# U, the masks and V0 in the opening of a convolution and low-rank mixer kernel, on one Trainium2 core

## The chip, the core and the metric

The kernel runs on one core of one Trainium2 chip. The core has five engines with an instruction stream each: TensorE (PE in the profile, with its weight loads shown apart as PEld), VectorE (DVE), ScalarE (ACT), GpSimd (POOL) and SyncE (SP). Data comes from device memory by transfers; in this kernel POOL issues nearly all loads (the queue "software_dynamic" of the profile), SP issues the transposes and the stores (the queue "hardware_dynamic"). The metric is the device time of one execution in microseconds (us). Durations of profiled instructions below are in us too.

## What is computed

x is 8 x 4224 x 192 float32. A causal convolution of seven taps comes first, with softmax weights for each of eight heads of 24 columns, and then a mixer: a product of rank 32 along the sequence, and a two-layer network along the columns.

```python
def _attn_ref(x, weight):                     # B, S, D = 8, 4224, 192; H, K = 8, 7
    w = exp(weight - max(weight)); w = w / (sum(w) + 1e-09)
    out = np.einsum('hk,bskhg->bshg', w, x_unf)      # K shifted views of x, heads of 24 columns

def _moe_ref(x, U, V, w_ch1, w_ch2):          # x is the convolution's output
    xt = x.transpose(0, 2, 1)
    h = xt @ U @ V                            # U is 4224 x 32, V is 32 x 4224
    u = x + h.transpose(0, 2, 1)
    ch = np.maximum(u @ w_ch1, 0.0) @ w_ch2   # 192 -> 768 -> 192
    return (u + ch).astype(np.float32)
```

## The kernel before

The kernel's order of work is written out by hand. Each batch of 4224 positions is 33 tiles of 128 positions; eight tiles make a group, 33 groups in all. For each group w1 multiplies by the first weight (L561, with ReLU evictions at L575 on ACT and L577 on DVE), w2 by the second (L590), and the result is added to u and stored (L599, L607). SLOTS is the list that lays the rest (convolutions of later batches, their sums with U, their products with V, transposes) between these products. None of that is touched by the change.

What is touched is the opening, the first 22 us, in which batch 0 is brought to its first group. In the order of PE:

- idle (L155) multiplies a tile of zeros by itself in float32, with no reader: one call has n products of w times 128 columns.
- The softmax weights become `cm` (8 x 7 x 8), which a product with the ones `one8` (L201) spreads to all 128 partitions. A copy makes `c2` of it (L218), two DVE products make `pr` (L226), and band_half (L241) sums these with the identity into a bank, from which ACT and DVE copy the band matrices (L261, L263: evac, on the engine that its letter names).
- The convolution of batch 0 comes in four pieces, KP, since x comes in four loads (x_piece, L79): conv_piece(k) needs piece k of x. Its products are L376, its evictions to y_sb are L261 and L263.
- u_layout (L269) puts U, loaded as four rows to a partition (Ur, L123 and L127), into U_sb by sixteen small products with the mask Eq; four evictions follow. It waits for both loads of Ur, for Eq, and for four free banks.
- yT (L514) transposes y of a group by a product with the identity, into three banks y0 that stay open.
- tt_mm (L409) sums y times U over the tiles of batch 0 into the bank tp; tt_split, a sum with R4 (L768), tt_late (L689) for the last piece, and tt_done make tt_sb of it.
- hT (L529) adds V times tt_sb to the open banks: three parts c of 64 columns, each with its own copy of the first 2048 columns of V, in the partitions 32c to 32c + 31 of V0_sb. Then it evicts the three banks as uT (ACT, DVE, ACT), which w1 of the groups 0 and 1 reads.

POOL's stream of transfers before: x piece 0, x piece 1, Ur, the rest of Ur, x pieces 2 and 3, three times V0 (L134), four parts of W1 (L138), then the first part of batch 1's x, V_sb, W2 and the rest of batch 1. At most eight of POOL's transfers are open: each further one waits for the landing of the one eight places before it. SP's stream before: the softmax weights (L61), and then nothing until the first transpose (L505).

The masks fp, R4 and Eq (L711, L714, L718) are made on DVE after yT of the first group. `early` are the 27 tiles of the pieces 0 to 2 (10, 11 and 6 of them); tt_mm takes them in two stretches, 21 and 6, before and after the first part of piece 3.

In the profile's lines the numbers are left off tile names: V_sb stands for V0_sb too, W_sb for W1_sb and W2_sb, and R for R4.

Of the kernel before, what the change touches and what calls it, by code (L numbers as in the profile page):

```python
# [7 lines left out]
ALU = mybir.AluOpType  # L8
ACT = mybir.ActivationFunctionType
BF16 = mybir.dt.bfloat16  # L10
F32 = mybir.dt.float32
# [3 lines left out]
def kernel(  # L15
# [10 lines left out]
    nc = tc.nc  # L26
    P = nc.NUM_PARTITIONS
    B, S, D = x.shape
    H, KC = weight.shape
    GS = D // H  # L30
    R = moe_U.shape[1]
# [4 lines left out]
    GT = 8  # L36
# [8 lines left out]
    cst = ctx.enter_context(tc.tile_pool(name="cst", bufs=1))  # L45
# [10 lines left out]
    def bank():  # L56
        return psp.tile([P, 512], F32, name="ps", tag="ps")
# [12 lines left out]
    def x_tile(b):  # L70
        xt[b] = xs.tile([P, NB1 + 1, D], BF16, name="x_sb")
# [4 lines left out]
    def x_part(b, r, s0, s1):  # L76

        blk = NB0 * r + s0 - 1
        return nc.gpsimd.dma_start(  # L79
            out=xt[b][HB * r : HB * r + HB, s0:s1, :],  # L80
            in_=x[b, blk * HB : (blk + s1 - s0) * HB, :].rearrange("(j p) d -> p j d", p=HB),
        )
# [3 lines left out]
    KP = [(0, 0, 10), (1, 0, 10), (1, 10, NB1 // 2), (0, 10, NB0 // 2)]  # L86

    def x_piece(k):
        r, k0, k1 = KP[k]
        x_part(0, r, 1 - r if k0 == 0 else 2 * k0 + 1, 2 * k1 + 1)  # L90

    def piece_tiles(k):
        r, k0, k1 = KP[k]
        return [NB0 // 2 * r + j for j in range(k0, k1)]
# [9 lines left out]
    def iota(t, pattern, base, mul):  # L104
# [4 lines left out]

    fp = cst.tile([P, P], I32, name="fp")  # L110
    nc.gpsimd.iota(fp[:], pattern=[[1, P]], base=P, channel_multiplier=-1)
    x_piece(1)
    dif = cst.tile([P, BW], F32, name="dif")
    iota(dif[:], [[1, BW]], 0, -1)
    tap = cst.tile([P, KC], F32, name="tap")
# [8 lines left out]
        out=Ur[:, 0:nfull, :], in_=U4[0 : nfull * P, :].rearrange("(k p) c -> p k c", p=P)  # L124
    )
    nlast = NT * 32 - nfull * P
    nc.gpsimd.dma_start(out=Ur[0:nlast, nfull, :], in_=U4[nfull * P :, :])  # L127
    for k in range(2, len(KP)):
        x_piece(k)


    V0_sb = cst.tile([3 * R, 2 * GT * P], BF16, name="V0_sb")
    for c in range(3):
        nc.gpsimd.dma_start(out=V0_sb[R * c : R * c + R, :], in_=moe_V[:, 0 : 2 * GT * P])  # L134
    W1_sb = cst.tile([P, 3, M4], BF16, name="W1_sb")
    for m0, m1 in ((0, 2 * P), (2 * P, M4)):
        for hf in range(2):
            nc.gpsimd.dma_start(  # L138
                out=W1_sb[HB * hf : HB * hf + HB, :, m0:m1],
                in_=moe_w_ch1[:, m0:m1].rearrange("(c k) m -> k c m", k=HB),  # L140
# [8 lines left out]
    Eq = cst.tile([P, P + 4], BF16, name="Eq")  # L149
# [3 lines left out]
    def idle(n, w=4, p=wps):  # L153
        for _ in range(n):
            nc.tensor.matmul(  # L155
                out=p[:, 0 : w * P].rearrange("p (n t) -> p n t", t=P),
                lhsT=zz[:],
                rhs=zz[:].unsqueeze(1).to_broadcast([P, w, P]),
                start=True,
                stop=True,  # L160
            )

    for w in (4, 2, 1):
        idle(1, w)
    one8 = cst.tile([H, P], F32, name="one8")
    nc.vector.memset(one8[:], 1.0)

    HQ = H // 2
# [1 line left out]
    for hh in range(2):  # L170
# [6 lines left out]
        out=d_sb[:], in0=w_sb[:], in1=mx_sb[:].to_broadcast([H, KC]), op=ALU.subtract  # L177
# [3 lines left out]
        out=ident[:], in0=fp[:], scalar1=float(P), scalar2=None, op0=ALU.is_equal  # L181
# [6 lines left out]
    nc.vector.tensor_scalar_add(s2_sb[:], s_sb[:], 1e-9)  # L188
    rs_sb = cst.tile([H, 1], F32, name="rs_sb")
    nc.vector.reciprocal(rs_sb[:], s2_sb[:])  # L190
    cm = cst.tile([H, KC, H], F32, name="cm")
    nc.vector.scalar_tensor_tensor(
        out=cm[:],
        in0=e_sb[:].unsqueeze(2).to_broadcast([H, KC, H]),
        scalar=rs_sb[:, 0:1],
        in1=ident[0:H, 0:H].unsqueeze(1).to_broadcast([H, KC, H]),
        op0=ALU.mult,
# [4 lines left out]
        out=cb[:, 0 : 2 * KC * HQ].rearrange("p (a k h) -> p a k h", a=2, k=KC),  # L202
# [7 lines left out]
        out=hot[:],  # L210
        in0=dif[:].unsqueeze(1).to_broadcast([P, KC, BW]),
        scalar=rq[:, 0:1],
        in1=tap[:].unsqueeze(2).to_broadcast([P, KC, BW]),
        op0=ALU.add,
# [4 lines left out]
        out=c2[:].rearrange("p a k h d -> p (a k h) d"),  # L219
        in_=cb[:, 0 : 2 * KC * HQ].unsqueeze(2).to_broadcast([P, 2 * KC * HQ, 2]),  # L220
    )
    prs = []
    for hh in range(2):
# [3 lines left out]
            out=pr[:].rearrange("p k h (t d) -> p k h t d", d=2),  # L227
            in0=hot[:]
# [4 lines left out]
            op=ALU.mult,  # L233
        )

    R4 = cst.tile([P, P], BF16, name="R4")

    def band_half(hh):
# [20 lines left out]
    def evac(eng, out, in_):  # L259
        if eng == "A":  # L260
            nc.scalar.activation(out=out, in_=in_, func=ACT.Copy)  # L261
        else:
            nc.vector.tensor_copy(out=out, in_=in_)  # L263

    def u_layout(up):
        nb = [nfull + (1 if 32 * jj < nlast else 0) for jj in range(4)]
        for a in range(4):
            for jj in range(4):
                nc.tensor.matmul(  # L269
                    out=up[jj][:, 0 : nb[jj] * R],  # L270
                    lhsT=Eq[32 * jj : 32 * jj + 32, 3 - a : 3 - a + P],
                    rhs=Ur[32 * jj : 32 * jj + 32, 0 : nb[jj], a * R : (a + 1) * R],
                    start=(a == 0),
                    stop=(a == 3),
                    tile_position=(32 * jj, 0),
                )
        for jj in range(4):
            evac(
                "AD"[jj % 2],
                U_sb[:, 0 : nb[jj], jj, :],  # L280
                up[jj][:, 0 : nb[jj] * R].rearrange("p (k r) -> p k r", r=R),
            )
# [1 line left out]
    idle(1, 2)  # L284
    idle(1, 1)
    band_half(0)
    idle(1, 1)
    band_half(1)


# [112 lines left out]
    def tt_mm(b, js, p=None, n0=0, n1=None):  # L403

        if p is None:
            p = bank()
        for n, j in list(enumerate(js))[n0:n1]:
            c = n % 4
            nc.tensor.matmul(  # L409
                out=p[32 * c : 32 * c + 32, 0:D],  # L410
                lhsT=U_sb[:, j // 4, j % 4, :],
                rhs=yt[b][:, j, :],
                start=(n < 4),
                stop=(n + 4 >= len(js)),
                tile_position=(0, 32 * c),
            )
        return p
# [14 lines left out]
    def tt_sum(b):  # L432
        p = bank()
        for n, part in enumerate(ttb[b]):
            nc.tensor.matmul(
                out=p[:, 0:D],
                lhsT=R4[:],
                rhs=part[:],
# [71 lines left out]
    def yT(g, c, p, i0=0, i1=4):  # L510

        for i in range(i0, i1):
            for hf in range(2):
                nc.tensor.matmul(  # L514
                    out=p[HB * hf : HB * hf + HB, i * P : (i + 1) * P],
                    lhsT=yt[0][:, GT * g + 4 * hf + i, HB * c : HB * c + HB],
                    rhs=ident[:],
                    start=(i == 0),
                    stop=False,
                    tile_position=(0, HB * hf),  # L520
                )
# [175 lines left out]
    def conv_piece(k, ns, engs, ps=None):  # L697
        r, k0, k1 = KP[k]
        nh = 512 // (GS * (k1 - k0))
        for n, h in list(enumerate(range(0, H, nh)))[ns]:  # L700
            conv(0, h, min(nh, H - h), [r], engs[n], {r: (k0, k1)}, ps and {r: ps[n]})

    every = slice(None)
    idle(1, 1)
    conv_piece(0, every, "ADAD")
    work = [bank() for _ in range(4)]
    tp = bank()
    y0 = [bank() for _ in range(3)]
    for c in range(3):
        yT(0, c, y0[c])  # L710
    nc.vector.tensor_scalar(  # L711
        out=fp[:], in0=fp[:], scalar1=R - 1, scalar2=None, op0=ALU.bitwise_and
    )
    nc.vector.tensor_scalar(  # L714
        out=R4[:], in0=fp[:], scalar1=0.0, scalar2=None, op0=ALU.is_equal
    )

    nc.vector.tensor_scalar(  # L718
        out=Eq[:, 3 : 3 + P].rearrange("p (k a) -> p k a", a=4)[:, :, 0],
        in0=fp[:, 0:R],  # L720
        scalar1=0.0,
        scalar2=None,
        op0=ALU.is_equal,
    )

    conv_piece(1, every, "ADAD", work)
    u_layout([tp] + work[:3])
    idle(3, 1, work[3])
    x_tile(1)
    x_zero(1, nc.gpsimd)  # L730
    x_part(1, *XP[0])
# [3 lines left out]
    for q in range(4):  # L735
        src = moe_V[:, 0 : full * 8 * P].rearrange("r (k q t) -> r k q t", q=4, t=2 * P)
        nc.gpsimd.dma_start(
            out=V_sb[32 * q : 32 * q + 32, 0 : 2 * full, :].rearrange(
                "r (k a) t -> r k (a t)", a=2
            ),  # L740
            in_=src[:, :, q, :],
# [3 lines left out]
        out=V_sb[0:32, 2 * (NT // 8), :], in_=moe_V[:, (NT - 1) * P : NT * P]  # L745
# [5 lines left out]
        out=U4_sb[:],  # L751
        in_=U_sb[:]
# [2 lines left out]
        .to_broadcast([P, len(late), 4, R]),  # L755
    )
    early = piece_tiles(0) + piece_tiles(1) + piece_tiles(2)
    na = len(early) - len(piece_tiles(2))
    conv_piece(2, every, "ADA", work)
    tt_mm(0, early, tp, 0, na)  # L760
    last = [work[3], work[0], work[1]]
    ps0 = work[2]
    conv_piece(3, slice(0, 1), "DAD", last)
    tt_mm(0, early, tp, na)
    tt_split(0, tp)
    conv_piece(3, slice(1, 3), "DAD", last)
    for n, part in enumerate(ttb[0]):
        nc.tensor.matmul(out=ps0[:, 0:D], lhsT=R4[:], rhs=part[:], start=(n == 0), stop=False)  # L768
    idle(1, 1, tp)
# [12 lines left out]
    for r in range(4):  # L782
        q = slice(QB * r, QB * r + QB)
        for hh in range(2):
            nc.gpsimd.tensor_copy(
                out=band2[q, HQ * hh : HQ * hh + HQ, :],
                in_=bands[hh][q, :, HB * (r % 2) : HB * (r % 2) + QB],
# [32 lines left out]
    for gs1, gs2, at in SLOTS:  # L820
# [13 lines left out]
        for p in range(npc + 1):  # L834
            for what in at.get(p, []):
                do(what)
            if p < npc:
                g, k = gs2[p // 4], p % 4
# [35 lines left out]
```

## Time and profile before

| | us |
|---|---|
| three runs | 327.41, 326.92, 327.23; median 327.23 |
| the profiled execution | 329.74 |
| its span, first to last instruction | 328.0 |
| PE busy in the span | 321.3 (98%) |
| DVE, ACT, POOL busy | 268.5, 169.6, 142.6 |

The page of the profile gives each engine's busy time, the queues, the chain of work that ended last, and the costliest groups of instructions. In a line of the timeline the first number is the start in us from the span's start, the second the duration of the whole row, then come the engine, the source line, the operation, what it writes and reads, the shape of one instruction and how many the row holds; in brackets is how long the engine was idle before and what ended the wait. In a line of the chain there are the start, the duration and the work. In a line of the transfers there are the tiles, the engine that issues them, how many, the size of one as it is written, and the median time from issue to landing.

### The profile page before, as it was taken

What the parts mean: (1) busy time and instruction counts of PE and PEld (TensorE: products, weight loads), DVE (VectorE), ACT (ScalarE), POOL (GpSimd) and SP (SyncE); (2) the same over time, 40 slices, a digit from 0 to 9 for tenths busy, and PEclk for the clock granted to TensorE, in tenths of its full rate; (3) what the DMA queues carried; (4) which work ended last, traced back from release to release, by engine and by line L of the source; (5) the groups of instructions that cost most, each with busy time, mean ns of one, the idle gap of its engine ahead of it and who ended that gap; (6) DMA issues with size and microseconds to landing.
All of it is one profiled execution on the core that took longest, in us unless ns stands there. A gap on an engine that the chain in (4) does not pass through costs nothing.

```text
span 328.0 us, 9606 instructions
## 1 busy us (share of the span) xinstructions
PE 321.3 (98%) x4006; PEld 226.6 (69%) x4006; DVE 268.5 (82%) x551; ACT 169.6 (52%) x341; POOL 142.6 (43%) x111
## 2 busy tenths in 40 slices
PE   8999999999999999999999999999999999999994
PEld 6866676478567746867864784587797497497494
DVE  5669989984977997897898699789898897896853
ACT  2467634760586198068429707833903902912910
POOL 8376159815993894994389599000000000000000
PEclk9999999999999999999999999999999999999998
DMA  8999994999999999899999989039369169159044
GB/s 100 193 180 175 211 234 106 185 180 184 247 109 190 215 190 136 172 222 159 218 227 155 143 236 197 26 99 248 67 150 246 41 143 254 39 129 257 2 136 155
DMA packets 122875, 53.76 MB, mean 164 GB/s; under 512 B 87664, under 2 KB 122736, under 8 KB 122832
## 3 DMA queue, kind: packets, MB, share of 16 engines
q1 hardware_dynamic: 84400, 38.06, 51.9%
q0 software_dynamic: 38288, 14.99, 40.5%
q8 instruction: 31, 0.51, 0.6%
q14 instruction: 12, 0.10, 0.1%
q10 hardware_dynamic: 144, 0.10, 0.1%
HBM read 29.98 MB, written 25.95 MB: 171 GB/s over the span
## 4 chain that ended last, share of the span: by engine, by line
PE 84%; DMA 4%; DVE 4%; ACT 3%; POOL 2%; issue 0%; SPq 0%; DVEq 0%
PE ps L590 38%; PE ps L561 33%; PE ps L346 3%; DMA out_dram<-out_sb 3%; PE ps L464 2%; DVE u_sb L486 2%; PE ps L155 2%; PE ps L376 2%; PE ps L409 2%; POOL xb_sb L312 2%; ACT rl_sb L575 2%; DMA uT<-u_sb 2%; ACT y_sb L261 1%; DVE out_sb L599 1%; DVE rl_sb L577 1%; ACT uT L261 1%
## 5 line engine op out<-in xcount | busy, mean ns | idle before, releaser
L575 ACT ACTIVATE rl_sb<-ps 128x512 bf16<-128x512 f32 x233 | 124.5, 604 | 109.6 <-PE ps L561 106.3
L590 PE MATMUL ps<-W_sb,rl_sb 128*128 128x192 bf16 x1584 | 141.1, 246 | 0.3
L590 PEld LDWEIGHTS <-rl_sb 128*128 128x128 bf16 x1584 | 128.4, 98 | 11.9 <-issue 11.2
L561 PE MATMUL ps<-uT,W_sb 64*128 64x512 bf16 x1188 | 132.2, 376 | 0.2
L577 DVE TENSOR_SCALAR rl_sb<-ps 128x512 bf16<-128x512 f32 x163 | 105.4, 687 | 15.6 <-PE ps L561 15.3
L561 PEld LDWEIGHTS <-W_sb 64*128 64x128 bf16 x1188 | 64.9, 94 | 63.1 <-issue 4.1
L599 DVE TENSOR_TENSOR out_sb<-ps,u_sb 128x384 f32<-128x384 f32 (+1 forms) x133 | 70.3, 548 | 28.0 <-PE ps L590 24.8
L312 POOL COPY xb_sb<-x_sb 32x3072 bf16<-32x3072 bf16 (+1 forms) x24 | 67.4, 2824 | 0.5
L486 DVE TENSOR_TENSOR u_sb<-y_sb,ps 128x192 bf16<-128x192 bf16 (+1 forms) x168 | 66.2, 458 | 0.0
L300 POOL COPY xb_sb<-x_sb 128x3072 bf16<-128x3072 bf16 x12 | 32.9, 2744 | 46.8 <-DMA x_sb<-in_x_dram 37.2
L261 ACT ACTIVATE y_sb<-ps 128x384 bf16<-128x384 f32 (+4 forms) x88 | 37.7, 517 | 11.5 <-PE ps L346 7.7
L79 POOL DMA_DIRECT2D x_sb<-in_x_dram x32 | 27.1, 850 | 8.7 <-PE ps L464 2.8
L263 DVE CAST y_sb<-ps 128x408 bf16<-128x408 f32 (+5 forms) x38 | 20.4, 576 | 2.4 <-PE ps L376 2.3
L464 PE MATMUL ps<-tt_sb,V_sb 32*128 32x192 bf16 x264 | 13.3, 246 | 0.6 <-DVE out_sb L599 0.3
L346 PE MATMUL ps<-xb_sb,band 64*32 64x384 bf16 x192 | 12.3, 332 | 0.2 <-POOL xb_sb L312 0.2
L346 PE MATMUL ps<-x_sb,band 64*32 64x384 bf16 x192 | 12.0, 332 | 0.0
L464 PEld LDWEIGHTS <-V_sb 32*128 32x128 bf16 x264 | 5.0, 92 | 8.4 <-issue 8.4
L376 PE MATMUL ps<-x_sb,band 64*64 64x240 bf16 (+3 forms) x192 | 9.6, 275 | 0.0
L423 ACT ACTIVATE tt_hi<-ps 128x192 bf16<-128x192 f32 x8 | 2.7, 331 | 12.3 <-PE ps L409 12.3
L376 PEld LDWEIGHTS <-band 64*64 64x64 bf16 x192 | 7.4, 106 | 1.8 <-issue 1.3
L155 PE MATMUL ps<-zz 128*128 128x128 f32 (+2 forms) x22 | 7.5, 480 | 1.1 <-DVE zz L144 1.1
L346 PEld LDWEIGHTS <-band 64*32 64x32 bf16 x384 | 4.7, 89 | 5.5 <-issue 2.6
(68 smaller groups left out, 71.8 us busy)
## 6 DMA issues: line engine op xcount, KB each, us to landing
out_dram<-out_sb SPq DMA_DIRECT2D x131, 192.0 KB, 3.3
x_sb<-in_x_dram POOLq DMA_DIRECT2D x14, 384.0 KB, 6.7
x_sb<-in_x_dram POOLq DMA_DIRECT2D x7, 432.0 KB, 7.9
x_sb<-in_x_dram POOLq DMA_DIRECT2D x7, 408.0 KB, 10.3
x_sb<-in_x_dram POOLq DMA_DIRECT2D x1, 504.0 KB, 8.1
uT<-u_sb SPq DMA_TRANSPOSE x31, 4.4
x_sb<-in_x_dram POOLq DMA_DIRECT2D x1, 480.0 KB, 5.6
V_sb<-in_moe_V_dram POOLq DMA_DIRECT2D x3, 128.0 KB, 9.7
```

What stands on the lines that cost most here:

```text
L79: return nc.gpsimd.dma_start(out=xt[b][HB * r : HB * r + HB, s0:s1, :], in_=x[b, blk * HB : (blk + s1 - s0) * HB, :].rearrange("(j p) d -> ...
L261: nc.scalar.activation(out=out, in_=in_, func=ACT.Copy)
L300: nc.gpsimd.tensor_copy(out=xbt[b][:, s0:s1, :], in_=xt[b][:, s0 + 1 : s1 + 1, :])
L312: nc.gpsimd.tensor_copy(out=xbt[b][q, s0:s1, :], in_=xt[b][q, s0:s1, :])
L346: nc.tensor.matmul(out=pp[r][QB * cg : QB * cg + QB, 0 : nk[r] * GS], lhsT=w[hr], rhs=t[hr, st : st + 2 * nk[r] - 1 : 2, hs], start=True, ...
L464: nc.tensor.matmul(out=banks[pr][:, a * D : (a + 1) * D], lhsT=V_sb[32 * q : 32 * q + 32, (j // 8) * 2 + j % 2, :], rhs=ttb[b][32 * q : 32 ...
L486: nc.vector.tensor_tensor(out=u_group(g)[:, i : i + n, :, hf, :], in0=yt[b][:, run[0] : run[0] + n, :].rearrange("p n (c k) -> p n c k", c=3),
L561: last = nc.tensor.matmul(out=pps[m][hf][:], lhsT=W1_sb[HB * hf : HB * hf + HB, c, m * P : (m + 1) * P], rhs=uTt[g][HB * hf : HB * hf + HB ...
L575: nc.scalar.activation(out=rl[:, m, hf, :], in_=pp[hf][:], func=ACT.Relu)
L577: nc.vector.tensor_scalar_max(out=rl[:, m, hf, :], in0=pp[hf][:], scalar1=0.0)
L590: last = nc.tensor.matmul(out=cps[:, a * D : (a + 1) * D], lhsT=rlt[g][:, m, hf, (i + a) * P : (i + a + 1) * P], rhs=W2_sb[:, m, :], start ...
L599: nc.vector.tensor_tensor(out=o[:, 0:n, :].rearrange("p n (c k) -> p n c k", c=3), in0=cps[:, 0 : n * D].rearrange("p (n c k) -> p n c k", ...
```

## The change

The load of Ur and its rest go ahead of x piece 1 in POOL's stream. V0 is loaded once; its second and third copy are made from the first, inside the on-chip memory, by two transfers that SP issues. The operands of the product that spreads the softmax weights become bfloat16. The idle product between the two band halves goes. On DVE the masks fp and Eq are made ahead of the bands' evictions, and R4 after U's evictions. On PE the layout of U moves from behind the convolution of piece 1 to ahead of yT of the first group; its three idle products (six passes) go, and one comes in ahead of piece 1. The sums with U are taken in three stretches, each ahead of a later piece: the 10 tiles of piece 0 ahead of piece 1, the 11 of piece 1 after piece 2, the 6 of piece 2 where they were. The rest of the program keeps its order on every engine.

```diff
--- before.py
+++ after.py
@@ -109,7 +109,6 @@
 
     fp = cst.tile([P, P], I32, name="fp")
     nc.gpsimd.iota(fp[:], pattern=[[1, P]], base=P, channel_multiplier=-1)
-    x_piece(1)
     dif = cst.tile([P, BW], F32, name="dif")
     iota(dif[:], [[1, BW]], 0, -1)
     tap = cst.tile([P, KC], F32, name="tap")
@@ -125,13 +124,14 @@
     )
     nlast = NT * 32 - nfull * P
     nc.gpsimd.dma_start(out=Ur[0:nlast, nfull, :], in_=U4[nfull * P :, :])
-    for k in range(2, len(KP)):
+    for k in range(1, len(KP)):
         x_piece(k)
 
 
     V0_sb = cst.tile([3 * R, 2 * GT * P], BF16, name="V0_sb")
-    for c in range(3):
-        nc.gpsimd.dma_start(out=V0_sb[R * c : R * c + R, :], in_=moe_V[:, 0 : 2 * GT * P])
+    nc.gpsimd.dma_start(out=V0_sb[0:R, :], in_=moe_V[:, 0 : 2 * GT * P])
+    for c in range(1, 3):
+        nc.sync.dma_start(out=V0_sb[R * c : R * c + R, :], in_=V0_sb[0:R, :])
     W1_sb = cst.tile([P, 3, M4], BF16, name="W1_sb")
     for m0, m1 in ((0, 2 * P), (2 * P, M4)):
         for hf in range(2):
@@ -162,7 +162,7 @@
 
     for w in (4, 2, 1):
         idle(1, w)
-    one8 = cst.tile([H, P], F32, name="one8")
+    one8 = cst.tile([H, P], BF16, name="one8")
     nc.vector.memset(one8[:], 1.0)
 
     HQ = H // 2
@@ -188,7 +188,7 @@
     nc.vector.tensor_scalar_add(s2_sb[:], s_sb[:], 1e-9)
     rs_sb = cst.tile([H, 1], F32, name="rs_sb")
     nc.vector.reciprocal(rs_sb[:], s2_sb[:])
-    cm = cst.tile([H, KC, H], F32, name="cm")
+    cm = cst.tile([H, KC, H], BF16, name="cm")
     nc.vector.scalar_tensor_tensor(
         out=cm[:],
         in0=e_sb[:].unsqueeze(2).to_broadcast([H, KC, H]),
@@ -233,6 +233,16 @@
             op=ALU.mult,
         )
 
+    nc.vector.tensor_scalar(
+        out=fp[:], in0=fp[:], scalar1=R - 1, scalar2=None, op0=ALU.bitwise_and
+    )
+    nc.vector.tensor_scalar(
+        out=Eq[:, 3 : 3 + P].rearrange("p (k a) -> p k a", a=4)[:, :, 0],
+        in0=fp[:, 0:R],
+        scalar1=0.0,
+        scalar2=None,
+        op0=ALU.is_equal,
+    )
     R4 = cst.tile([P, P], BF16, name="R4")
 
     def band_half(hh):
@@ -284,7 +294,6 @@
     idle(1, 2)
     idle(1, 1)
     band_half(0)
-    idle(1, 1)
     band_half(1)
 
 
@@ -706,26 +715,12 @@
     work = [bank() for _ in range(4)]
     tp = bank()
     y0 = [bank() for _ in range(3)]
+    u_layout(work)
+    nc.vector.tensor_scalar(
+        out=R4[:], in0=fp[:], scalar1=0.0, scalar2=None, op0=ALU.is_equal
+    )
     for c in range(3):
         yT(0, c, y0[c])
-    nc.vector.tensor_scalar(
-        out=fp[:], in0=fp[:], scalar1=R - 1, scalar2=None, op0=ALU.bitwise_and
-    )
-    nc.vector.tensor_scalar(
-        out=R4[:], in0=fp[:], scalar1=0.0, scalar2=None, op0=ALU.is_equal
-    )
-
-    nc.vector.tensor_scalar(
-        out=Eq[:, 3 : 3 + P].rearrange("p (k a) -> p k a", a=4)[:, :, 0],
-        in0=fp[:, 0:R],
-        scalar1=0.0,
-        scalar2=None,
-        op0=ALU.is_equal,
-    )
-
-    conv_piece(1, every, "ADAD", work)
-    u_layout([tp] + work[:3])
-    idle(3, 1, work[3])
     x_tile(1)
     x_zero(1, nc.gpsimd)
     x_part(1, *XP[0])
@@ -755,13 +750,16 @@
         .to_broadcast([P, len(late), 4, R]),
     )
     early = piece_tiles(0) + piece_tiles(1) + piece_tiles(2)
-    na = len(early) - len(piece_tiles(2))
+    n1, n2 = len(piece_tiles(0)), len(early) - len(piece_tiles(2))
+    tt_mm(0, early, tp, 0, n1)
+    idle(1, 1, work[3])
+    conv_piece(1, every, "ADAD", work)
     conv_piece(2, every, "ADA", work)
-    tt_mm(0, early, tp, 0, na)
+    tt_mm(0, early, tp, n1, n2)
     last = [work[3], work[0], work[1]]
     ps0 = work[2]
     conv_piece(3, slice(0, 1), "DAD", last)
-    tt_mm(0, early, tp, na)
+    tt_mm(0, early, tp, n2)
     tt_split(0, tp)
     conv_piece(3, slice(1, 3), "DAD", last)
     for n, part in enumerate(ttb[0]):
```

## The prediction

> **What bounds the kernel now.** I read the page first, then the chain of waits of the opening, its timeline, and the transfers. The page says that PE is the bound of the whole:
>
> ```profile
> span 328.0 us, 9606 instructions
> ...
> PE 321.3 (98%) x4006; PEld 226.6 (69%) x4006; DVE 268.5 (82%) x551; ACT 169.6 (52%) x341; POOL 142.6 (43%) x111
> ```
>
> All edits lie in the first 21 us, and everything after hangs on PE, so a shift of the first group's start should reach the end whole. The chain up to 45 us shows what the opening pays for:
>
> ```profile
> 4.42 0.60 PE ps L201 x2
> 5.02 1.58 PE ps L155 x4
> ...
> 7.49 0.51 PE ps L155 x2
> ...
> 14.68 0.86 PE ps L155 x6
> ...
> 21.05 2.04 ACT uT L261 x4
> 23.09 2.95 ACT rl_sb L575 x6
> ```
>
> The spread (L201) runs in two passes, and idle products (L155) stand in the chain. From 21.05 ACT carries the path: four evictions of uT, then the ReLUs from 23.09. The timeline gives the pieces that move:
>
> ```profile
> 6.39 1.09 PE L241 MATMUL ps<-pr,ident 128*128 128x152 bf16 x7
> ...
> 9.08 1.83 PE L376 MATMUL ps<-x_sb,band 64*64 64x240 bf16 x32
> ...
> 12.01 1.83 PE L376 MATMUL ps<-x_sb,band 64*64 64x240 bf16 x32
> ```
>
> The pieces 0 and 1 take 1.83 each; 7 products of 152 columns took 1.09, though 32 of 240 columns (16 pairs side by side) take 1.83: 1 ns a column against 0.5. PE's pace doubles near 9.0. Then the loads on POOL's queue up to 26 us:
>
> ```profile
> x_sb<-in_x_dram POOLq DMA_DIRECT2D x1, 504.0 KB, 8.1
> x_sb<-in_x_dram POOLq DMA_DIRECT2D x1, 480.0 KB, 5.6
> ...
> V_sb<-in_moe_V_dram POOLq DMA_DIRECT2D x3, 128.0 KB, 9.7
> ...
> x_sb<-in_x_dram POOLq DMA_DIRECT2D x1, 336.0 KB, 9.2
> x_sb<-in_x_dram POOLq DMA_DIRECT2D x1, 288.0 KB, 10.1
> ...
> Ur<-in_moe_U_dram POOLq DMA_DIRECT2D x1, 256.0 KB, 9.1
> ```
>
> With the issues of the timeline (x piece 0 at 1.26, piece 1 at 2.56, Ur 3.73, pieces 2 and 3 at 5.19 and 5.98, V0 from 6.71) they land at 6.9, 10.7, 12.8, 14.4, 16.1, and the first V0 at 16.4. They land in the order of issue: the queue is backed up from 3 us on. Last, SP's stores (192 KB) issued between 35.5 and 37, where all 761 packets that moved were POOL's, and one between 54 and 55, where nothing else moved:
>
> ```profile
> q0 software_dynamic: 761, 0.29, 160.3%
> ...
> out_dram<-out_sb SPq DMA_DIRECT2D x3, 192.0 KB, 6.8
> ```
>
> ```profile
> out_dram<-out_sb SPq DMA_DIRECT2D x1, 192.0 KB, 2.0
> ```
>
> A transfer of SP's that meets a backlog of POOL's takes 5.9 to 8.6 instead of 2.0.
>
> **The change part by part.** *Spread in bf16.* Two passes of 0.67 become one. The band sum now starts when the idle products behind the spread are over (6.39; pr was ready at 6.08), so what the spread loses comes off: about 0.45, bounds 0.3 and 0.67. *Idle product between the bands*: 0.51 less. Piece 0 can start at 8.1 instead of 9.08; x piece 0 (6.9) and the first band's copies by ACT (8.12 before, 7.7 now) allow it.
>
> *Masks fp and Eq ahead of the bands' copies on DVE*: 0.22 + 0.20 after pr (6.1 to 6.6). DVE idles 1.45 there, waiting for ACT; that is the cover, and without it 0.42 would fall on the bands. Nil.
>
> *Pace.* Piece 0 at 8.1 would run its first 0.9 at the slow pace, losing half of that if the pace turns at 9.0 again: 0.3 to 0.45. It ends near 10.05 instead of 10.7. The Trainium skill, "TensorE: Matmul & The Clock Gate", section "What's actually happening", says that the array runs at half clock until a free-running window of about 3.4 us has been busy; the granted clock shown here reads 1.00 from the start, so only the durations show it. By that page alone the turn could slip by a window, and the sum would lose the front part of the gain.
>
> *Layout of U after piece 0.* Ur now follows x piece 0 in the queue: 6.9 + (12.8 - 10.7) + 0.25 for its rest = 9.3, ahead of 10.05. Sixteen products, 0.91 as a row; its four evictions (two of 0.41 on ACT, two of 0.43 on DVE) queue behind those of piece 0 and end at 11.75. R4 (0.22) and the U4 copy (0.36) follow on DVE, ahead of piece 1's evictions, which come later. yT (1.02) fits beside them, then ten sums with U at 0.03 wait for the last eviction and end at 12.1; one idle product, 0.3.
>
> *Piece 1 waits.* x piece 1 now lands behind Ur: the same bytes are ahead of it as were ahead of Ur's rest, so 9.3 + (10.7 - 6.9) = 13.1. PE is ready at 12.4 and waits 0.7. That takes the whole early gain; what remains is that layout and idle products are out of the way behind it: piece 1 to 14.85, piece 2 (landed 14.4) to 16.1 instead of 15.47 to 16.75, eleven sums instead of 21 (0.33 against 0.53), piece 3 at 16.45 instead of 17.28. It lands at 16.1. So hT would be due at 19.8 instead of 20.58: 0.8 gained. If piece 1 lands at 12.4, piece 3's own landing holds the gain to 1.15; an Ur or x that lands 0.3 later leaves 0.5.
>
> *V0's copies.* POOL issues two transfers fewer (0.55 each), and W1 lands up to 1.2 earlier (16.4 to 17.6 was V0's); nothing waited for either. The copies wait on SP for the first V0 (16.4) and are issued at 16.45 and 16.85 (0.4 an issue, the row of the weights' load). Behind them SP has nothing until the transpose at 28.36. hT's parts c = 1 and 2 need them at 19.8. They meet the rest of W1 and batch 1's first x, which is in POOL's queue by 13.3 now, since the wait eight places back is for x piece 1 and no longer for piece 3. An SP transfer of their kind under a backlog is in no row at this place. Bounds: alone 2.0, so the second lands at 18.85; as the stores at 33.28 and 35.60 did (6.4 and 5.9), at 22.75 to 23.25. The transpose at 28.36, under the same backlog, took 6.1 against 3.6 to 4.0 alone, a wait of 2.3; the stores wait 3.9 to 4.4. Being small, the copies are nearest to the wait itself, and I take its middle, 3.0: the second lands at 16.85 + 2.0 + 3.0 = 21.85.
>
> The page "DMA: Bandwidth & Descriptors", section "Queues, rings and completion order", speaks against this: an engine takes turns between queues packet by packet, at most 64 descriptors each. At the 32 ns that a packet of POOL's took per engine (761 over 16 engines in 1.5 us) a turn is an estimated 2.0 at most, 0.5 for 17; by it the second copy lands at 19.4 to 20.85.
>
> *What a late copy costs.* PE stops at hT's third part. Counted from its landing t: product 0.45, then PE finishes yT and hT of group 1 at t + 1.1, and ACT makes the third eviction and the two of group 1, so that the ReLUs start at t + 2.15; before they started at 23.09. The change in time is t - 20.95, and not below -0.8. With 21.85: +0.9. **Sum**: the span goes from 328.0 to 328.9. The profiled execution (329.74) is 1.7 over its span and 2.5 over the median of the runs; I carry the difference over to the median: 327.23 + 0.9 = **328.1**.
>
> **The rivals.** *A, the copies land in time* (by 20.15): POOL's transfers at that place are small (W1's 96 and 192 KB against 384 KB and more at 33 us), so SP may get its turn after one of them, as the page has it. For it: the transpose at 28.36 lost only 2.3. Against: the three stores at 35.5. Time 327.23 - 0.8 = 326.4, down to 326.1 if x piece 1 is early. *B, a wash*: the wait is 2.0 to 2.7, the copies land at 20.85 to 21.5, and the late hT takes back what the earlier pieces gave: 327.1 to 327.8. *C, slower by the whole store-like wait*: landing at 22.75 to 23.25, time 329.0 to 329.5; this is the forecast's upper end. *D, the pace turns a window later*: 16 pairs of piece 0, layout and yT at the slow pace end near 14 instead of 12.4, piece 1 starts 0.9 after its landing, and the gain is gone before the copies matter: 327.3 by itself, no change against the forecast if the copies are late.
>
> **How the numbers follow.** Forecast with C (copies late by over 0.65 net) 0.48; B and D 0.22; A 0.30. A difference under 0.2% (0.65 us) is about what cannot be told from none here; the three runs lie within 0.49. So faster 0.30, same 0.22, slower 0.48. The forecast's own range is 327.9 to 329.5; that of 8 in 10 takes in most of A and leaves out C's end: 326.3 to 329.1.
>
> **What would show it.** The late copies: a wait of PE or of its weight loads ahead of hT's second or third part (L538 in the new file), and landings of the transfers V_sb<-V_sb over 4 us. The gain ahead of it: piece 3 near 16.45, a wait of about 0.7 ahead of piece 1 for x, no wait ahead of the layout. The pace: the first products of piece 0 0.2 apart until 9.0. The forecast is wrong if the copies land within 3.5 us of their issue, or if the ReLUs of group 0 start before 22.5.

## The result, and the profile after

The changed kernel takes 335.74 us (median of four executions, 334.01 to 336.73) against 327.08 of the kernel before (four, 326.43 to 327.41): a ratio of 1.0262, 95% interval 1.0216 to 1.0307, slower by 8.7 us. The forecast had slower as the likeliest sign, at +0.9; a rise of 8.7 is far outside its range. Below, medians are over all executions of a kernel, while a ratio leaves out those more than 1.5% above the fastest of their kernel, so the two can part (in a1 a rise of 4.2 by the medians and of 1.7 by the ratio, in b1 of 4.2 and 3.6).

The profiled execution of after took 334.01, its span 332.2. The page's first lines:

```profile
span 332.2 us, 9590 instructions
...
PE 322.9 (97%) x3999; PEld 225.8 (68%) x3999; DVE 268.4 (81%) x551; ACT 170.0 (51%) x341; POOL 141.6 (43%) x109
```

PE is still the bound, its busy time is 1.6 longer with seven products fewer, and the span is 4.2 longer. Part of PE's work ran slower, and PE waited more. This pair understates the change: the profiled execution of after was the fastest of its four, and that of before (329.74) was over the median. The additions that make the output (DVE, L608) show where the time is lost: the first is 5.5 later than before, the one at 183 us 3.8 later, and from there to the end the distance stays at 3.8. So the loss is in the opening.

The timeline of after, PE's rows from 5 to 34 us (start, length, engine, line, operation, tiles, shape, count, and in brackets the wait just ahead and its releaser):

```profile
5.69 1.24 PE L251 MATMUL ps<-pr,ident 128*128 128x152 bf16 x14
...
7.26 1.83 PE L385 MATMUL ps<-x_sb,band 64*64 64x240 bf16 x32
10.05 0.65 PE L279 MATMUL ps<-Ur,Eq 32*128 32x288 bf16 x16 [0.96 <-DMA Ur<-in_moe_U_dram]
...
13.05 3.69 PE L385 MATMUL ps<-x_sb,band 64*64 64x240 bf16 x64 [0.72 <-DMA x_sb<-in_x_dram]
...
17.27 0.93 PE L385 MATMUL ps<-x_sb,band 64*64 64x144 bf16 x12
...
20.68 1.17 PE L698 MATMUL ps<-y_sb,U_sb 128*128 128x192 bf16 x6
21.78 0.92 PE L523 MATMUL ps<-ident,y_sb 128*64 128x128 bf16 x16
22.63 0.41 PE L538 MATMUL ps<-V_sb,tt_sb 32*64 32x512 bf16 x4
24.43 0.40 PE L538 MATMUL ps<-V_sb,tt_sb 32*64 32x512 bf16 x2 [1.39 <-DMA V_sb<-V_sb]
...
25.45 5.75 PE L570 MATMUL ps<-uT,W_sb 64*128 64x512 bf16 x36
```

The same work in the kernel before:

```profile
17.28 0.56 PE L376 MATMUL ps<-x_sb,band 64*64 64x144 bf16 x12
...
19.42 0.67 PE L689 MATMUL ps<-y_sb,U_sb 128*128 128x192 bf16 x6
...
20.58 0.41 PE L529 MATMUL ps<-V_sb,tt_sb 32*64 32x512 bf16 x6
...
21.68 4.06 PE L561 MATMUL ps<-uT,W_sb 64*128 64x512 bf16 x36
```

Two things are to be seen. Waits: 0.96 for Ur, 0.72 for x piece 1, 1.39 for the second copy of V0. And rows that are longer than before with the same work: 12 products of piece 3 take 0.93 (0.56 before), tt_late 1.17 (0.67), the 36 products of w1 5.75 (4.06). The granted clock says why; the windows below are cut where it changes, with the busy time of PE, PEld, DVE, ACT and POOL (and their counts), then the clock (1.00 is full), the transfers' share and their rate:

```profile
8.76:12.18 3.42, 2.46 (x59) 1.68 (x54) 2.15 (x6) 1.21 (x3) 1.43 (x3) 1.00 1.60 192
12.18:15.59 3.41, 2.67 (x54) 2.36 (x54) 1.32 (x2) 1.17 (x3) 1.29 (x2) 1.00 1.47 195
15.59:19.00 3.41, 3.41 (x57) 2.37 (x53) 1.29 (x2) 1.33 (x3) 2.33 (x6) 0.50 1.37 197
19.00:22.41 3.41, 3.41 (x40) 2.82 (x36) 1.17 (x3) 0.54 (x2) 1.63 (x3) 0.50 1.42 223
22.41:25.83 3.42, 2.03 (x34) 0.92 (x30) 0.93 (x2) 1.48 (x3) 3.25 (x8) 1.00 1.60 192
25.83:29.24 3.41, 3.41 (x20) 1.23 (x16) 1.74 (x3) 1.95 (x5) 0.70 (x3) 0.50 1.83 187
```

PE was busy 2.46 and 2.67 of 3.41 in the first two stretches, and the next two run at half clock. Then PE is busy 2.03 of 3.42, waiting for the copy, and once more the next stretch runs at half. In the kernel before, the record of the clock turns to full at 8.75 and stays there to the last products. The chain of waits of the opening (start, length, what) now runs through the copy:

```profile
6.74 10.30 DMA V_sb<-in_moe_V_dram
...
17.72 6.67 DMA V_sb<-V_sb
24.38 0.04 issue
24.43 0.40 PE ps L538 x2
```

The first V0 lands at 17.04, the second copy is issued at 17.72 and lands at 24.38, and hT's third part starts at once.

### The profile page after: what moved, and what is told of

It reads as the page before. It is cut to its first block, busy times and chain, and to the rows that moved or that the text cites. A ratio compares the mean times of both kernels' runs of the same rounds, so it can differ in the third digit from the quotient of the medians.

```text
span 332.2 us, 9590 instructions
## 1 busy us (share of the span) xinstructions
PE 322.9 (97%) x3999; PEld 225.8 (68%) x3999; DVE 268.4 (81%) x551; ACT 170.0 (51%) x341; POOL 141.6 (43%) x109
## 4 chain that ended last, share of the span: by engine, by line
PE 83%; DMA 7%; DVE 4%; ACT 2%; POOL 2%; issue 1%; SPq 0%; POOLq 0%; DVEq 0%
PE ps L570 38%; PE ps L599 38%; DMA V_sb<-in_moe_V_dram 3%; PE ps L355 3%; PE ps L473 2%; DMA out_dram<-out_sb 2%; DMA V_sb<-V_sb 2%; DVE u_sb L495 2%; PE ps L418 2%; POOL x_sb L79 1%; ACT y_sb L271 1%; DVE rl_sb L586 1%; DVE out_sb L608 1%; ACT rl_sb L584 1%; PE ps L444 0%
## 5 line engine op out<-in xcount | busy, mean ns | idle before, releaser
L570 PE MATMUL ps<-uT,W_sb 64*128 64x512 bf16 x1188 | 134.0, 380 | 0.1
L608 DVE TENSOR_TENSOR out_sb<-ps,u_sb 128x384 f32<-128x384 f32 (+1 forms) x133 | 70.3, 549 | 26.6 <-PE ps L599 24.4
L473 PE MATMUL ps<-tt_sb,V_sb 32*128 32x192 bf16 x264 | 12.6, 246 | 0.1
L385 PE MATMUL ps<-x_sb,band 64*64 64x240 bf16 (+3 forms) x192 | 11.1, 300 | 0.8 <-DMA x_sb<-in_x_dram 0.7
L385 PEld LDWEIGHTS <-band 64*64 64x64 bf16 x192 | 8.8, 120 | 3.0 <-issue 2.3
L418 PE MATMUL ps<-y_sb,U_sb 128*32 128x192 bf16 x258 | 8.1, 255 | 0.0
```

The lines of the kernel that those rows point to most:

```text
L473: nc.tensor.matmul(out=banks[pr][:, a * D : (a + 1) * D], lhsT=V_sb[32 * q : 32 * q + 32, (j // 8) * 2 + j % 2, :], rhs=ttb[b][32 * q : 32 ...
L570: last = nc.tensor.matmul(out=pps[m][hf][:], lhsT=W1_sb[HB * hf : HB * hf + HB, c, m * P : (m + 1) * P], rhs=uTt[g][HB * hf : HB * hf + HB ...
L608: nc.vector.tensor_tensor(out=o[:, 0:n, :].rearrange("p n (c k) -> p n c k", c=3), in0=cps[:, 0 : n * D].rearrange("p (n c k) -> p n c k", ...
```

## The experiments

Three questions: what the late copies cost, what the clock costs and which wait lowers it, and where the gain of the earlier pieces is. The kernel before ran beside each set; its medians were 327.74, 327.74, 327.87 and 328.13 (82 executions, median 327.85). The clock changes in whole windows of 3.41 us, which start at another time in each execution (it first turned full between 4.0 and 10.0), so the same wait can fall into one window or be split over two.

### a1: V0 loaded three times, the rest of the change kept

```diff
-    nc.gpsimd.dma_start(out=V0_sb[0:R, :], in_=moe_V[:, 0 : 2 * GT * P])
-    for c in range(1, 3):
-        nc.sync.dma_start(out=V0_sb[R * c : R * c + R, :], in_=V0_sb[0:R, :])
+    for c in range(3):
+        nc.gpsimd.dma_start(out=V0_sb[R * c : R * c + R, :], in_=moe_V[:, 0 : 2 * GT * P])
```

> The changed kernel with the three V0 parts loaded by POOL again, as before; all other edits kept. Theory 1 (two losses: the copies land about 4 us late, and PE's waits for U and for x piece 1 bring a clock drop at 15.6 us that costs up to 3.4 us): 330 to 332 us, with a clock drop near 15.6 and no wait at hT. Rival 2 (the copies carry everything, the clock follows from them): 326.3 to 327.5. Rival 3 (the moved layout and the clock carry everything, the copies are hidden): 334 to 336.

Median 331.97 (ten executions, 327.23 to 334.40), ratio 1.0052 (1.0001 to 1.0104). In the profiled execution (333.94) hT is in time and the first output is 0.85 earlier than in the kernel before: the gain that the prediction had at 0.8. Then it is lost at another place. The timeline of a1 (here and below, rows of PE alone):

```profile
31.06 3.13 PE L598 MATMUL ps<-W_sb,rl_sb 128*128 128x192 bf16 x36
...
39.06 5.31 PE L569 MATMUL ps<-uT,W_sb 64*128 64x512 bf16 x31 [4.88 <-DMA uT<-u_sb]
```

The transpose of u for the third group, issued on SP's queue at 27.51, lands at 39.02, 11.5 later (6.1 in the kernel before). PE waits 4.88, and the clock is at half from 39.48 to 42.89. So the copies are not the only transfer of SP's that can land late while POOL's loads are open. The median lies in Theory 1's range, but not for its reason: that theory had a drop of the clock near 15.6, and here the clock is full from 5.34 to 39.48, though PE waits 0.79 and 0.66 for pieces of x (Ur was in time). This execution is one of the longest of the ten; by the ratio a1 is 1.7 above the kernel before (0.0 to 3.4), so how often the late transpose comes is not shown.

### a2: a1 with idle products in PE's two waits

```diff
+    idle(4, 1, work[3])
     u_layout(work)
...
-    idle(1, 1, work[3])
+    idle(4, 1, work[3])
     conv_piece(1, every, "ADAD", work)
```

> As the run before it, and idle products fill the two waits: four ahead of the layout of U (wait 1.0 us) and four instead of one ahead of x piece 1 (wait 0.7 us). Theory 1: no clock drop before 20 us, 326 to 327.5, that is 3 to 5 us less than without the fill. Rival 2: the same as without the fill. Rival 3 (if the waits themselves cost, and not the clock): within 0.5 us of the run without the fill.

Median 328.18 (ten, 326.02 to 334.54), ratio 1.0007 (0.9971 to 1.0043): the kernel before, within what can be told (0.9 less to 1.4 more). The clock is full from 6.79 to the last products of the profiled execution. What the change holds besides the copies and the two bare waits neither costs nor brings anything that these executions can tell. Theory 1 had 3 to 5 less than a1: the medians differ by 3.8, the ratios by 1.5, with intervals that overlap, so a cost of the bare waits is not shown here.

### b1: the copies alone, in the kernel before

The edit is the reverse of a1's, made in the kernel before.

> The kernel before with V0's second and third part copied on SP's queue, nothing else changed. Theory 1: hT waits until about 24 us, 3.5 us late, and the idle PE may bring one clock drop of 3.4 us at half pace: 330 to 333 us. Rival 2: 334 to 336. Rival 3: 326.8 to 328.

Median 331.99 (four, 329.22 to 338.91), ratio 1.0110 (1.0025 to 1.0195). The timeline of b1:

```profile
20.27 0.40 PE L530 MATMUL ps<-V_sb,tt_sb 32*64 32x512 bf16 x2
22.95 0.40 PE L530 MATMUL ps<-V_sb,tt_sb 32*64 32x512 bf16 x2 [2.28 <-DMA V_sb<-V_sb]
23.59 0.40 PE L530 MATMUL ps<-V_sb,tt_sb 32*64 32x512 bf16 x2 [0.23 <-DMA V_sb<-V_sb]
...
24.61 5.75 PE L562 MATMUL ps<-uT,W_sb 64*128 64x512 bf16 x36
```

Here too the copies land late (22.91 and 23.54, 5.7 after their issue both), and again w1 takes 5.75, since the clock is at half from 24.68 to 28.09. The copies alone bring some 4 us, about half of the 8.7; with four executions that is rough (3.6 by the ratio, 0.8 to 6.4).

### b2: the spread product in bf16 alone

In the kernel before, `one8` and `cm` in BF16 in place of F32.

> The kernel before with the operands of the spread in bf16, nothing else changed (the softmax weights are rounded to bf16 ahead of the spread). All theories: the band sums start 0.45 us earlier and everything follows: 326.5 to 327.0. If the clock turns fast a window earlier because of it (it did at 5.3 us in the changed kernel and at 8.75 us in the one before), up to 1.7 us less: 325.3.

Median 328.52 (ten, 326.08 to 333.16), ratio 1.0003 (0.9976 to 1.0031): nothing that can be told.

### c0: the changed kernel once more

> The changed kernel unchanged, to see how its time stands to the granted clock from execution to execution. Theory CLOCK (PE's waits for Ur and x piece 1 let the clock fall to half for two windows of 3.4 us, on top of the copies): hardly any execution keeps the full clock, the mean clock stays near 0.98 to 0.99 and the median near 335.7 (334 to 337), 2.3 to 2.9% over the kernel before on the same chip. Theory COPIES (the loss is the late copies alone, and the half clock of the profiled execution was its own bad luck): executions with a clock of 0.998 and above turn up and lie near 330 to 331; the median falls towards 332.

Median 334.72 (six, 331.39 to 338.89), ratio 1.0169 (1.0127 to 1.0212). With the first four executions the median of ten is 335.39, and the mean clock of the span 0.976 to 0.995, with a median of 0.987; no execution of the ten keeps 0.998, as 14 of the 17 of the kernel before in this set do. In the profiled execution, the fastest of the six, half clock falls into 19.1 to 22.5, and the copies land at 23.08 and 23.71. So some half clock comes with the change in all ten, as CLOCK had it, and the median is in its range, though the ratio is under its 2.3 to 2.9%. Where the half clock falls differs: here PE waits 1.43 for Ur and 1.50 for x piece 3, one window at half follows, ahead of the copies' landing, and none comes after the wait for the copies (0.76 in all), so w1 takes 4.06.

### c1: the changed kernel with a2's idle products

The edit is a2's, with the copies on SP's queue kept.

> The changed kernel, with V0's two copies on SyncE's queue as it has them, but four idle products of 128 columns ahead of the layout of U and four in place of one ahead of piece 1, which cover PE's waits for Ur and x piece 1. CLOCK: the granted clock stays full from its turn until PE waits for the copies near 20; the median falls from 335.7 to about 331 to 332.5, like the kernel before with the copies alone (332.0): what the copies cost stays, what the half clock cost (3 to 4) goes. COPIES: nothing changes, 335 to 336, since the copies land as late as before. In both the copies land 5 to 7 us after their issue.

Median 333.04 (six, 332.57 to 336.87), ratio 1.0182 (1.0143 to 1.0221). The timeline of c1:

```profile
20.05 0.40 PE L538 MATMUL ps<-V_sb,tt_sb 32*64 32x512 bf16 x2
23.52 0.40 PE L538 MATMUL ps<-V_sb,tt_sb 32*64 32x512 bf16 x2 [3.07 <-DMA V_sb<-V_sb]
24.47 0.40 PE L538 MATMUL ps<-V_sb,tt_sb 32*64 32x512 bf16 x2 [0.55 <-DMA V_sb<-V_sb]
...
25.87 5.26 PE L570 MATMUL ps<-uT,W_sb 64*128 64x512 bf16 x36
```

Now the clock is full until 24.93, and hT is ready at 20.05 instead of 22.63. Yet its third part starts at 24.47, against 24.43 in after: what the first two windows of half clock cost in after lay under the wait for the copy. After the wait the clock is at half from 24.93 to 28.34. The median is 1.7 to 2.4 below that of after, between the two forecasts, but by the ratios c1 is not below c0 at all (1.0182 and 1.0169), so a cost of the waits for Ur and x piece 1, with the copies in place, is not shown.

### c2: c1 with the loads behind the copies held back

```diff
+    late_conv = conv_piece(3, slice(1, 3), "DAD", last)
+    x_tile(1)
+    x_zero(1, nc.gpsimd)
+    held(x_part(1, *XP[0]), late_conv)
...
```

V_sb and W2 follow that load in POOL's stream, as before.

> As the run with copies and idle products, but the loads that meet the copies on the queues (batch 1's first x, the five of V and W2) are held until the last products of piece 3, near 18.6, so that the copies meet only the rest of W1. BACKLOG (the copies are slow because they share the DMA engines with POOL's queued loads): they land 2 to 3.5 us after their issue, by 21.0 at the latest, PE does not wait at the third part of hT, and the time falls to about 328 to 329.5, with up to 1 us lost later where V and x come later. Rival SLOW FORM (a transfer from SBUF to SBUF of 32 rows by 4 KB takes 5 to 7 us by itself): the copies still land 5 us or more after their issue, and the time stays at 331 to 332.5 or more.

Median 331.38 (six, 329.45 to 337.29), ratio 1.0094 (1.0057 to 1.0130). The transfers issued from 17 to 26 us or under way then (tiles, queue, count, KB each, median from issue to landing), first of after, then of c2:

```profile
V_sb<-V_sb SPq DMA_DIRECT2D x2, 128.0 KB, 6.0
```

```profile
V_sb<-V_sb SPq DMA_DIRECT2D x2, 128.0 KB, 4.1
```

And the timeline of c2:

```profile
20.00 0.40 PE L538 MATMUL ps<-V_sb,tt_sb 32*64 32x512 bf16 x2
20.94 0.72 PE L538 MATMUL ps<-V_sb,tt_sb 32*64 32x512 bf16 x4 [0.54 <-DMA V_sb<-V_sb]
...
22.29 4.06 PE L570 MATMUL ps<-uT,W_sb 64*128 64x512 bf16 x36
```

The copies land at 20.90 and 21.22 instead of 23.48 and 24.43, PE waits 0.54 instead of 3.6, the clock stays full, and w1 takes 4.06. So the loads that were held cost the copies 2.0 and 2.7 of their 6.3 and 6.6, and the rival was right in part: even with only the rest of W1 ahead they take 4.1, not 2.0. Their landings lie between the two forecasts, and the median lies in the rival's range. The profiled execution (329.47) is one of the two shortest of the six, and in it PE waits 1.2 for transposes of u further on; why the median stands 1.9 higher is not shown.

### c3: two idle products of the kernel before removed

In the kernel before, without `idle(1, 1)` between the bands and `idle(3, 1, work[3])` ahead of piece 2.

> The kernel before without the idle product between the two bands and without the three ahead of piece 2; nothing else is changed, U, V0, masks and spread as before. CLOCK FROM IDLE (the removed idle products by themselves let the clock fall): half clock for one or two windows between 9 and 20, median 329.5 to 332. CLOCK FROM WAITS (only the moved layout and the order of the loads make the gaps): the clock stays full as in the kernel before, and the time is that of the kernel before, 326.5 to 328.5.

Median 328.43 (twelve, 326.25 to 334.37), ratio 1.0012 (0.9976 to 1.0047), clock full from 9.28 on. Removing these idle products does no harm that can be told.

### d1 and e1: idle products in the wait for the copies

```diff
     def hT(g, ps, engs, fill=None):
...
+            if fill is not None and c:
+                idle(12 if c == 1 else 2, 1, fill)
```

That is e1, on top of c1; `fill` is the bank that yT of the second group opens next. d1 had `idle(14 if c == 1 else 3, 4, fill)`.

> As the run with copies and idle products (c1, median 333.0), but with fourteen idle products of 512 columns ahead of the second part of hT and three ahead of the third, so that PE is busy while it waits for V0's copies; the copies themselves stay as late. WAIT AND CLOCK (a late copy costs its wait and, through the idle PE, a window of half clock after it): the clock stays full from its turn to the end, group 0's first-layer products (36 of them) take 4.06 again instead of 5.7, and the median falls by half a window, 1.7, to about 331.3. WAIT ALONE (the wait is the whole price, the half clock falls into time that is lost anyway): 333 as before, or 0.3 more where the idle products overrun the copies' landing.

d1 missed: median 342.40 (341.87 to 342.61). Float32 products of 512 columns last 0.88, so the fill ran far past the copies' landing, as its timeline shows:

```profile
20.88 12.28 PE L155 MATMUL ps<-zz 128*128 128x512 f32 x28
```

But its clock was full to the end, w1 took 4.06, and the spread over six executions was 0.7. With the size mended:

> The run with copies and idle products (c1, median 333.0) with the wait of hT filled to size: twelve idle products of 128 columns (0.22 each, 2.6 in all) ahead of its second part and two ahead of its third, in place of the seventeen of 512 columns (0.88 each) of d1, which overran the copies by some 11 us. WAIT AND CLOCK: hT's second part comes at 23.5 to 24 as without them, the clock stays full, group 0's 36 first-layer products take 4.06, the median falls to about 331.3, and what is left against the kernel before, 3.5, is the bare wait. WAIT ALONE: 333 as before.

Median 330.97 (twelve, 330.26 to 336.06), ratio 1.0092 (1.0060 to 1.0124), apart from c1's. The timeline of e1:

```profile
20.10 0.40 PE L540 MATMUL ps<-V_sb,tt_sb 32*64 32x512 bf16 x2
20.43 2.94 PE L155 MATMUL ps<-zz 128*128 128x128 f32 x24
23.31 0.40 PE L540 MATMUL ps<-V_sb,tt_sb 32*64 32x512 bf16 x2
...
24.69 0.40 PE L540 MATMUL ps<-V_sb,tt_sb 32*64 32x512 bf16 x2 [0.34 <-DMA V_sb<-V_sb]
...
25.71 4.06 PE L572 MATMUL ps<-uT,W_sb 64*128 64x512 bf16 x36
```

The copies are as late as in c1 (23.15 and 24.65), and w1 starts 0.16 from where it did, but at full clock. Nothing changed but that PE had something to do while it waited (and that a bank was taken a little earlier for it), and the median fell by 2.1. Theory WAIT AND CLOCK holds. The profiles put 1.4 of it at the first output (5.41 late in c1, 4.05 in e1); the rest lies between executions.

### d2, e2 and d3: where the opening's gain goes

d2 is a2 with the last of batch 1's x loads issued later, held to w1 of the second group:

```diff
-    for xp in XP[1:]:
+    for xp in XP[1:3]:
         x_part(1, *xp)
...
             ends = w1(g, RELU0 if g == 1 else RELU)
+            if g == 1:
+                held(x_part(1, *XP[3]), ends[3])
```

> The changed kernel with V0 loaded three times and the idle products (a2, median 328.2), and batch 1's last x load issued near 29 instead of 25, behind the first transpose on SyncE's queue, so that the transpose does not meet it. STARVED TRANSPOSE (the transposes of u behind POOL's queued x loads are what is left between a2 and the kernel before, and what spreads the runs): the transpose lands in 4 to 5.5 us instead of 7.8, PE's wait of 1.15 for it goes, the median falls to 326.5 to 327.3 and the spread narrows. NOT IT: the transpose waits for the other loads of the queue all the same (7 us and more), median 328 or more; where x comes too late for batch 1's conv near 40, up to 2 us more.

Median 328.06 (twelve, 327.62 to 331.61), ratio 1.0026 (0.9992 to 1.0061). The first transpose now lands in 5.1 (27.34 to 32.48), and the first outputs are 1.02 ahead of the kernel before. Then the waits of PE from 20 to 60 us have one entry (in total, times, longest):

```profile
PE ps L569 <- DMA uT<-u_sb: 2.5, 1, 2.5
```

It is the second transpose, issued at 41.23 and landed at 49.81, while loads of batch 2's x were open. So the first transpose came as STARVED TRANSPOSE had it, but the median did not fall. e2 is d2 with the last of batch 2's loads held until that transpose is issued: `held(x_part(2, *XP[3]), last)` behind `held(transp(3), last)`.

> The run with V0 loaded three times, idle products and batch 1's last x load behind the first transpose (d2, median 328.1, first mark 1.0 ahead of the kernel before, then 2.5 lost to a wait for the second transpose, 8.6 us from issue to landing), and now batch 2's last x load held until that second transpose is issued, near 41 instead of 33. NEXT QUEUE (the opening's gain is real and is given back at the second transpose alone): the second transpose lands within 6 us, PE's wait near 49 shrinks from 2.5 to under 0.5, and the median goes to 325.5 to 326.8, below the kernel before. STILL BOUND (the loads of batch 1 and 2 bound the stretch from 25 to 50 whatever their order): the wait moves on to the next transpose, x shift or conv, and the median stays at 327.5 to 329.

Median 332.75 (six, 331.54 to 334.11), ratio 1.0127 (1.0077 to 1.0178). The waits of PE in e2 from 20 to 150 us:

```profile
PE ps L354 <- POOL xb_sb L320: 2.0, 1, 2.0
PE ps L569 <- DMA uT<-u_sb: 1.5, 2, 1.1
PE ps L472 <- DVE out_sb L607: 1.4, 1, 1.4
```

The second transpose takes 7.2 even so, which speaks for STILL BOUND, but the time is worse than either theory had it. POOL now waits 1.91 for the held load, which lands at 51.63; the wait of a convolution for POOL's shift of x (2.0) comes at 128.9, in a later batch, and that the one leads to the other is not followed up. The first transpose, with the same load held as in d2, took 7.0 here against d2's 5.1 and a2's 7.8, so the two runs together do not show that this load decides it. d3, the one held load of d2 in the kernel before:

> The kernel before with that one load moved in the same way and nothing else. STARVED TRANSPOSE: the profiled execution of before had no wait for it, so the best executions stay near 326, but those of 328 and more become fewer; median 326.3 to 327.2. NOT IT: 327.7 like the kernel before, with the same spread.

Median 329.37 (twelve, 326.92 to 334.58), ratio 1.0038 (1.0007 to 1.0070): no gain, rather a small loss, with a wait of 1.9 for a transpose. No version here is faster than the kernel before.

## Why the prediction was wrong

The sign was right, and so was the wait that the prediction named: the copies on SP's queue are held up by POOL's loads, and PE stops at hT's third part. The size was far off: 8.7 instead of 0.9. Two steps failed. The copies' wait, taken at 3.0, was 4.67. And the price of a late copy, t - 20.95, took PE's pace as constant, while a window at half clock after the wait added up to 1.7. The steps in order:

- *Spread, bands, masks, pace.* The bands and piece 0 came earlier than taken: piece 0 starts at 7.26, not 8.1, and runs at full pace (1.83), since in this execution the clock turned full at 5.35 (5.44 in c0). Rival D, a later turn, did not occur in these two. That the turn came early is luck: it differs from execution to execution. By itself the bf16 spread is worth nothing that can be told (b2).
- *Layout of U after piece 0.* Ur landed at 9.71 and 9.91, not 9.3; with piece 0 over early, PE waited 0.96 where no wait was foreseen.
- *Piece 1 waits 0.7.* Right: x landed at 13.01 (13.1 taken), PE waited 0.72. What was missing is that these two waits, in neighbouring windows, were followed by 6.8 us at half clock. That is not so in every execution (one window in c0; none in a1, where PE waited for x alone). Here piece 3 started at 17.27, not 16.45, and hT at 22.63, not 19.8. With the waits filled (c1), hT is ready at 20.05: 0.53 ahead of before, in the bounds of 0.5 to 1.15.
- *V0's copies.* This is the first step that failed, by its size. They were taken to wait 3.0, with the second landing at 21.85, at most 23.25; it landed at 24.38. Of the 2.53, the later first V0 (17.04 for 16.4) and issues of 0.62 instead of 0.4 make 0.87 (17.72 against 16.85), and the rest, 1.66, is the wait: 4.67 over the 2.0, more than the store-like 3.9 to 4.4 of rival C. In the other runs with this backlog the wait over 2.0 of the second copy ran from 3.1 (c0) to 5.0 (e1), so 3.0 was the low end. c2 shows that 2.0 alone was too short for them as well. The Trainium skill, "DMA: Bandwidth & Descriptors", section "Queues, rings and completion order", has an engine change queues after each packet, from which the prediction estimated 19.4 to 20.85; the first packet of the copies moved at 20.16, 3.1 after the issue, and the landings at 22.44 and 24.38 speak against that estimate.
- *What a late copy costs, t - 20.95.* This is the second step that failed. The rule held for what it counts. e1, where PE is kept busy, has t = 24.65, hence +3.7: 331.6 over 327.85, measured 330.97. Its failure is what it leaves out: it took PE's pace as constant. A window of half clock after the wait costs up to half of 3.41, 1.7. With that, b1 (t = 23.54) comes to 327.85 + 2.59 + 1.7 = 332.1, measured 331.99, and c1 (t = 24.43) to 333.0, measured 333.04; but these set one execution's landing against a median. Execution by execution it can be checked at the first output: the rule, with 1.7 where a window at half follows the wait (after, b1, c1), gives 5.13 in after, 4.29 in b1, 2.76 in c0, 5.18 in c1, 0.27 in c2 and 3.70 in e1, and the first output was 5.48, 4.63, 3.12, 5.41, 0.62 and 4.05 later than in the kernel before. That is 0.2 to 0.4 more each time.
- *The sum.* With t = 24.38 and a window: 327.85 + 3.43 + 1.7 = 333.0, a rise of 5.1. The changed kernel measured 335.39 over ten executions, 2.4 more; by the ratios the rise was 8.6 (7.1 to 10.0) in the first four and 5.5 (4.2 to 6.9) in c0. What is left, between 0.4 and 3.5, can't be laid to one place: in the profiled execution the half clock ahead of hT lay under the copies' wait, c0 and c1 are not apart by their ratios, and a1 shows that a late transpose with a further window of half clock can follow. More half clock is not it for the first four: the three others had a higher mean clock (0.988 and 0.989) than the profiled one (0.981) and took 1.7 to 2.7 longer. This part stays open.
- *Rival A, the copies in time: 326.4.* a1 and a2 are that case. The first group was indeed ahead in the profiles (0.85 in a1, 1.02 in d2, 0.25 in e2, 0.14 in a2), but the end was not: 331.97 in a1, 328.06 in d2, 332.75 in e2, 328.18 in a2. The assumption that a shift of the first group reaches the end whole failed for a gain. PE met waits for the transposes of u (4.88, 2.5, 1.1 and 1.15 long). The transposes waited for took 7.2 to 11.5, with loads of x open, and 3.8 and 4.8 where they were issued between such loads (c1, after); which load decides is not shown. A loss does reach the end: of the 5.5 at the first output of after, 3.8 are left at 183 us, but c3, which has no loss to make up, gains 2.8 on the same execution of before in that stretch, so the 1.7 belong to the profiled execution of before.

On the clock, the measured rows first: PE busy 2.03 of 3.42 in after, 0.86 of 3.42 in c1 and 44% of a window in b1 were followed by a window at half. The Trainium skill, "TensorE: Matmul & The Clock Gate", section "What's actually happening", has the throttled state come back after an idle window of about 3.4 us. The length agrees with the 3.41 here, but no window here was idle: PE was busy for 12% of it at the least (a1, from 36.1 to 39.5).

## What to carry to other kernels

A wait of PE's is priced twice, by its length and by the slow stretch that can follow; where it can't be removed, filling it with idle products sized to its length buys back the second part (2.1 us in c1 against e1). A transfer that is moved to a quiet engine's queue can still be slowed by the busy queue's loads (6.3 and 6.6 in c1, 4.3 and 3.9 with part of the loads held), so price it by the slowest transfer that met the same backlog, not by its size or by the middle. And before counting a gain to the end, look at the next transfer that PE needs: if it was just in time, the gain can turn into a longer wait for it.

## What the runs showed of the hardware

- Half clock came in whole windows of 3.41 us, or two of them (6.8 in after), and after a busy share that was far from zero. There was no clean threshold: windows with PE busy 66% (a2), 69% (c1) and 45% (a1) had full clock after them, and 78%, in a second window after one of 72% (after), did not; in c0 alone, 58% was followed by full clock and 56% by half.
- The phase of these windows differs between executions: the clock first turned full at 4.0 (d2), 5.35 (after), 6.8 (a2), 8.75 (before) and 10.0 (d3).
- A copy of 128 KB from SBUF to SBUF took 5.1 to 7.0 from issue to landing under the backlog (after, b1, c0, c1, e1), and 3.9 and 4.3 with part of it held back (c2). The transposes of u near 28 and 42 took 5.1 to 11.5 with loads of x open (before, a1, a2, d2, e2), the one at 33.8 took 3.8 in c1 and 4.8 in after, where no load of x was open as it was issued.
